# Talking-heads attention and an FFT feed-forward on one core: another order of work where the two stages meet

## The chip, the core and the metric

The kernel runs on one core of a Trainium2 chip. The core has five engines, each with a queue of its own: TensorE (matmuls, PE in the profile, with its weight loads apart as PEld), VectorE (DVE), ScalarE (ACT), GpSimd (POOL) and SyncE (SP), which here only issues transfers. They meet through semaphores. The metric is the device time of one execution in microseconds; of several executions the median counts.

## The reference

All data is float32, except the two feed-forward weights, which come as float64 and are turned into float32 by the kernel itself, bit by bit, on VectorE.

```python
# q, k, v: (8, 12, 448, 64); w_pre, w_post: (12, 12)
scores = scale * q @ k.transpose(0, 1, 3, 2)
scores = einsum('bhij,hg->bgij', scores, w_pre)
attn = softmax(scores)                    # max, exp, sum + 1e-9
attn = einsum('bhij,hg->bgij', attn, w_post)
x = heads_side_by_side(attn @ v)          # (8, 448, 768)

u = x + real(fft(fft(x, axis=1), axis=2))
un = (u - mean(u)) / sqrt(var(u) + 1e-6)  # along the last axis
out = u + relu(un @ w_ch1) @ w_ch2        # w_ch1: (768, 3072), w_ch2: (3072, 768)
```

## The kernel before

**Two stages.** `mix_phase` computes attention and the Fourier part and writes u to memory, into `u_scr` and `u_rev`. `ffn_phase` reads u back in tiles of 512 rows (seven of them, t = 0 to 6), normalises, and does the two products. Both products use a scheme of seven half-size products in place of eight (Strassen's), so each has seven operands per side: ub and w1t for the first, h and w2t for the second, in the order of `ORDER = (0, 4, 5, 1, 6, 2, 3)`. Some operands are sums of others: for ub the four differences in `total`, which come after the others.

**Attention** runs in 192 steps (TOT), 24 to each of the 8 batches. A step computes a pre-mix (L478, tile mx), the row maxima (L485), the exponentials (L492, tile PP), the scaling by the row sums on GpSimd (L502), the post-mix (L512, tile po) and a transpose on VectorE (L523, tile Pv). Which work goes with which step is written out by hand: `ORDERS` gives the order within even and odd steps, and the `AT_...` tables give the step in which each other piece is due. Six steps make a group of 112 rows, four groups a batch. For each group the products with v (L539; 56 matmul instructions for each of three parts, pr = 0, 1, 2) go from PSUM into XT, a tile with a single buffer, through four ScalarE copies a part (the helper's line L330, XT<-ms). In three of the four groups one or two columns of XT have no rows of their own; `done` clears them after the copies of the last part (L561, on GpSimd: 1, 2, 0 and 1 columns for groups 0 to 3). Six TensorE transposes (L572) then turn XT, and two ScalarE copies bring the result into X.

**Folds.** The Fourier part begins with sums and differences of the X of two groups, on GpSimd (L593 to L614): 8 operations for the first pair of groups of a batch and 12 for the second. They go into a list, `folds`, of which each step takes one or two, after its scaling on GpSimd. What is left when the steps are over is taken by `fold_rest`, which `ffn_phase` calls. The products that follow (L637, L653) come later; those of the last batch are dealt out between the products of the first feed-forward tile (`next_part`).

**The seam.** Before the first product (L954), tile t = 0 has to be made ready, for four slices of 128 rows (x = 0 to 3):
- `stats`: means and variances on VectorE (L900, L901);
- `power`: the inverse square roots ("roots"), four small operations on GpSimd (L905 to L908);
- `norm`: un = (u - mean) times root, on ScalarE (L916), two buffers for four slices;
- `turn`: six TensorE transposes a slice (L925) into two PSUM tiles psQ of two buffers, y = 0 and 1, and a ScalarE copy of each (L927) into ub;
- `total`: the four differences of ub on VectorE (L933), and then the stores of all seven ub on SyncE (L937), which later rounds read back;
- the loads of w1t (L881) and w2t (L885) on SyncE, seven of 384 KB each.

**What sets the order.** A planner orders each engine's queue when the program is built, by the place of an instruction in the program and by the time at which its own model takes its inputs to be ready. In a `manual_schedule` region the engines named keep the order in which the program emits their instructions. Where a region's instructions fall among those of another region, though, is left to the planner, and so is the order on engines that a region doesn't name. Attention is one region, for TensorE, VectorE, ScalarE and GpSimd. `stats(0)`, `power(0)` and `fold_rest` are a second, for TensorE, VectorE and GpSimd. Everything behind them is a third, for TensorE and VectorE only: ScalarE's part (un, the copies to ub) and SyncE's transfers are placed by the planner, which may put them between instructions of attention.

Of the kernel before, what the change touches and what calls it, by code (L numbers as in the profile page):

```python
# [16 lines left out]
P = 128  # L17
# [30 lines left out]
TOT = B * GS  # L48
# [5 lines left out]
MG = 4  # L54
# [45 lines left out]
NK = DM // 2 // P  # L100
# [35 lines left out]
def _ap(t: bass.AP, offset: int, dims) -> bass.AP:  # L136
    return bass.AP(tensor=t.tensor, offset=t.offset + offset,
                   ap=[list(d) for d in dims])
# [6 lines left out]
def _row(t: bass.AP) -> int:  # L145
    return t.ap[0][0]
# [144 lines left out]
def mix_phase(ctx, tc, rest, ident, q, k, v, w_pre, w_post, u_scr, u_rev, wts):  # L291
# [6 lines left out]
    nc = tc.nc  # L298
# [28 lines left out]
    pend, folds, later = [], [], []  # L327

    def copy(eng, out, in_):
        (nc.scalar.copy if eng == "a" else nc.vector.tensor_copy)(out=out, in_=in_)  # L330

    def flush():
        while pend:
            pend.pop(0)[1]()
# [7 lines left out]
    def ms_tile():  # L342
        return ms[-1]()
# [115 lines left out]
    def emit_gather(T):  # L459

        Kr = pkr.tile([P, 2, S], F32, name="Kr", tag="Kr")
        Sb = blocks[T // BS]["Sb"]
        row = _row(Sb)
        for z in range(2):
            for x in range(2):
                p0 = MG + 4 * (T % BS) + 2 * z + x
                nc.sync.dma_start(  # L467
                    out=Kr[64 * x:64 * x + KR, z, :],
                    in_=_ap(Sb, p0 * row, [[RS * row, 2 * R], [S, 6], [1, S]]))
        steps[T]["Kr"] = Kr  # L470
# [25 lines left out]
    def emit_scale(T):  # L496
        PP, den = steps[T]["PP"], steps[T]["den"]
        rcp = psm.tile([P, 2], F32, name="rcp", tag="rcp")
        nc.vector.tensor_scalar(rcp[:, :], den[:, :], 1e-9, None, op0=ALU.add)  # L499
        nc.vector.reciprocal(out=rcp[:, :], in_=rcp[:, :])  # L500
        for x in range(2):
            nc.gpsimd.tensor_scalar(PP[:, x, :], PP[:, x, :], rcp[:, x:x + 1], 1.0,  # L502
                                    op0=ALU.mult, op1=ALU.mult)
# [24 lines left out]
    def emit_av(g, pr):  # L528

        st = batches[g["b"]]  # L530
        Pv = g["Pv"]
        rp = _row(Pv)
        nu = GT * 4
        pss = [ms_tile() for _ in range(2)]
        for jb in range(C7):
            for x in range(2):
                for y in range(2):
                    i = 2 * pr + x
                    nc.tensor.matmul(  # L539
                        pss[y][64 * x:64 * x + 64, :nu * R],  # L540
                        st["v", pr][64 * y:64 * y + 64, x, jb * D:(jb + 1) * D],
                        _ap(Pv, 64 * y * rp + 32 * jb + R * i,
                            [[rp, 64], [HS, nu], [1, R]]),
                        start=(jb == 0), stop=(jb == C7 - 1))
        if pr == 0:
            g["XT"] = pxt.tile([P, 6, XW], F32, name="XT", tag="XT")
        XT = g["XT"]
        rx = _row(XT)
        first, sg, none = PLACE[g["gi"]]

        def done(y):
            rs = _row(pss[y])
            for e in range(2):

                o = MG + first + sg * NB * e
                dst = _ap(XT, (3 * y + pr) * XW + o, [[rx, P], [sg * RS, R], [sg, RS]])
                src = _ap(pss[y], 60 * e, [[rs, P], [1, R], [R, RS]])
                copy(ENG["AV"][y], dst, src)
            if y == 1 and pr == 2:
                for o in none:  # L560
                    nc.gpsimd.memset(XT[:, :, MG + o:MG + o + 1], 0.0)  # L561
        return [lambda y=y: done(y) for y in range(2)]

    def emit_x(g):
# [173 lines left out]
    def take(kind, s):  # L738
        large = 0
        while fill[kind] and fill[kind][0][0] <= s:  # L740
            fn = fill[kind].pop(0)[2]
            if kind == "none":
                large += bool(fn())
            elif kind == "full":
                flush()
                pend.extend((1, e, None) for e in fn())
            else:
                room(2)
                evs, n = fn()
                pend.extend((1, e, n) for e in evs)  # L750
        return large

    s = int(min(v_[0][0] for v_ in fill.values()))
    ET = mybir.EngineType
    with tc.manual_schedule(engines={ET.PE, ET.DVE, ET.Activation, ET.Pool}):
        while s <= TOT - GS + AT_X[-1]:
            old = len(later)
            n = take("none", s)
            ahead, now = 0 <= s + LM < TOT, 0 <= s < TOT
            for op in ORDERS[s % 2]:  # L760
                if op == "flush":
                    flush()
                elif op in fill:
                    take(op, s)
                elif op == "conv":
                    if s >= 4:
                        wts.deal(1)
                elif op == "gather":
                    if 0 <= s + LG < TOT:
                        if any(e[2] is not None and e[2] <= (s + LG) // BS for e in pend):  # L770
                            flush()
                        emit_gather(s + LG)
                elif op == "scale":
                    if ahead:
                        emit_scale(s + LM)
                    for _ in range(old):
                        later.pop(0)()
                    for _ in range(min(len(folds), 1 if n and s > 3 else 2)):
                        folds.pop(0)()
                elif op in ("post", "turn"):  # L780
                    if now:
                        (emit_postmix if op == "post" else emit_turn)(s)
                elif ahead:
                    (emit_premix if op == "pre" else emit_max if op[0] == "m"
                     else emit_exp)(s + LM, *map(int, op[3:]))
            s += 1
        flush()
        wts.deal(1000)
# [26 lines left out]
ORDER = (0, 4, 5, 1, 6, 2, 3)  # L815
# [5 lines left out]
def ffn_phase(ctx, tc, rest, ident, u_scr, u_rev, wts, ub_scr, out, fold_rest,  # L821
# [4 lines left out]
    nc = tc.nc  # L826
# [23 lines left out]
    def ps_tile(key):  # L850

        n = taken[key] = taken[key] + 1
        more = len(pps) > 3 and key != "Q" and n % 3 == 0
        return pps[3 if more else "QPR".index(key)].tile(
            [P, 512], F32, name="ps" + key, tag="ps" + key, bufs=1 if more else 2)
# [5 lines left out]
    us, ubs, w1, w2 = {}, {}, {}, {}  # L861
# [21 lines left out]
    def load_w2(c, i):  # L883
        w2[i] = pw2.tile([P, FM, DH], F32, name="w2t", tag="w2t")
        nc.sync.dma_start(out=w2[i][:, :, :], in_=wts.w2[c][i])  # L885
# [5 lines left out]
    UB = {(0, 0): 0, (0, 1): 6, (1, 0): 1, (1, 1): 2}  # L891
# [19 lines left out]
    def norm(t, x):  # L911
        if x == 0:
            for i in (0, 6, 1, 2, 4, 5, 3):
                new_ub(t, i)
        uns[x] = pun.tile([P, DM], F32, name="un", tag="un")
        nc.scalar.activation(uns[x][:, :], us[t][:, x, :], ACTF.Identity,  # L916
                             bias=mvs[t][:, x, 2:3], scale=mvs[t][:, x, 1:2])

    def turn(t, x):
        un = uns.pop(x)  # L920
        for y in range(2):
            ps = ps_tile("Q")
            for c in range(NK):
                cc = NK * y + c
                nc.tensor.transpose(ps[:, c * P:(c + 1) * P],  # L925
                                    un[:, cc * P:(cc + 1) * P], ident[:, :])
            nc.scalar.copy(  # L927
                out=ubs[t, UB[y, x // 2]][:, :, (x % 2) * P:(x % 2 + 1) * P],
                in_=ps[:, :NK * P].rearrange("p (c n) -> p c n", n=P))

    def total(t, n):
        o, a, b = ((4, 6, 0), (5, 2, 4), (6, 2, 6), (3, 1, 5))[n]
# [112 lines left out]
    with tc.manual_schedule(engines={ET.PE, ET.DVE}):  # L1045
        for x in range(NT2):
            norm(0, x)
            turn(0, x)
        for n in range(4):
            total(0, n)  # L1050
        for i in ORDER:
            load_w2(0, i)
        for n in range(NC * NTB):
            c, t = divmod(n, NTB)

            if c + 1 < NC and 0 <= t - (c == 0) < NK + FM:
                wts.add(c + 1, t - (c == 0))
            wts.deal(0)
            if c == 0 and t + 2 < NTB:
                load_u(t + 2)  # L1060
            second(n, first(n))
            wts.deal(1000)
            if n == 0:
                assert not parts
                rest.close()
                pu.append(pool("pu2", side="right"))
                beside.close()
                pps.append(pool("ppy", space=bass.MemoryType.PSUM))
# [61 lines left out]
```

## Time and profile before

The median of three runs is 2419.3 us (2418.86 to 2423.73). The profiled execution:

| | |
|---|---|
| span | 2415.9 us |
| TensorE busy | 2357.9 us (98%) |
| VectorE / ScalarE / GpSimd busy | 1545.1 / 799.1 / 792.6 us |
| attention's last post-mix (L512) begins | 834.1 us |
| the first feed-forward product, L954 | 860.6 us |

The profile's page gives totals over the whole span. The seam is some 25 us of 2416, about 1%, so it doesn't show in the totals. It has to be read from the views that keep the order of time: the timeline of one engine in a window, the chain of waits in that window, and the table of windows, which also gives TensorE's granted clock. In a timeline each row is a start in us, a duration in us, engine, line, operation, tiles written and read, and a count where like instructions follow each other; a bracket gives the time that the engine had stood idle, and what released it.

The group rows for the work that the change touches (time in all, mean in ns, and the idle time before them):

| work | line | engine | count | busy us | mean ns |
|---|---|---|---|---|---|
| clearing of XT | L561 | GpSimd | 32 | 3.2 | 118 |
| folds: pairs | L593 | GpSimd | 64 | 64.4 | 1015 |
| un | L916 | ScalarE | 28 | 28.2 | 1030 |
| transposes of un | L925 | TensorE | 168 | 25.2 | 278 |
| copies to ub | L927 | ScalarE | 56 | 24.8 | 482 |
| totals of ub | L933 | VectorE | 28 | 29.1 | 1043 |

### The profile page before, as it was taken

What the parts mean: (1) busy time and instruction counts of PE and PEld (TensorE: products, weight loads), DVE (VectorE), ACT (ScalarE), POOL (GpSimd) and SP (SyncE); (2) the same over time, 40 slices, a digit from 0 to 9 for tenths busy, and PEclk for the clock granted to TensorE, in tenths of its full rate; (3) what the DMA queues carried; (4) which work ended last, traced back from release to release, by engine and by line L of the source; (5) the groups of instructions that cost most, each with busy time, mean ns of one, the idle gap of its engine ahead of it and who ended that gap; (6) DMA issues with size and microseconds to landing.
All of it is one profiled execution on the core that took longest, in us unless ns stands there. A gap on an engine that the chain in (4) does not pass through costs nothing.

```text
span 2415.9 us, 54667 instructions
## 1 busy us (share of the span) xinstructions
PE 2357.9 (98%) x21680; PEld 1592.4 (66%) x21680; DVE 1545.1 (64%) x3103; ACT 799.1 (33%) x2059; POOL 792.6 (33%) x1293
## 2 busy tenths in 40 slices
PE   6999999999999899999999999999999999999999
PEld 3555555555555477676777777777777777777776
DVE  3878879789897757775667356635664457533333
ACT  4776767676677532321110110110110111111110
POOL 3587877878776531120111011101110011000000
PEclk9999999999999999999999999999999999999999
DMA  6665555656554556336444444534442644353331
GB/s 147 177 177 167 183 170 163 188 164 187 170 175 160 175 194 208 131 139 241 142 137 146 150 146 129 162 124 159 146 153 93 200 133 141 121 170 112 118 118 53
DMA packets 168620, 372.50 MB, mean 154 GB/s; under 512 B 36750, under 2 KB 90022, under 8 KB 168366
## 3 DMA queue, kind: packets, MB, share of 16 engines
q1 hardware_dynamic: 129038, 260.22, 32.5%
q0 software_dynamic: 33760, 107.40, 15.2%
q8 instruction: 173, 2.83, 0.5%
q10 hardware_dynamic: 5568, 1.38, 0.3%
q14 instruction: 81, 0.66, 0.1%
HBM read 211.98 MB, written 74.34 MB: 119 GB/s over the span
## 4 chain that ended last, share of the span: by engine, by line
PE 89%; DMA 4%; DVE 2%; SPq 2%; POOL 2%; ACT 1%; issue 1%; ACTq 0%; DVEq 0%; POOLq 0%
PE psP L954 18%; PE psP L1010 18%; PE psR L954 9%; PE psR L1010 9%; PE mx L478 6%; PE ms L539 5%; PE ms L451 5%; PE po L512 5%; PE psQ L1010 5%; PE psQ L954 5%; DMA Kr<-Sb 3%; PE ms L653 2%; SPq L467 1%; PE ms L426 1%; PE ms L637 1%; PE ms L572 1%
## 5 line engine op out<-in xcount | busy, mean ns | idle before, releaser
L954 PE MATMUL psP<-ub,w1t 128*128 128x256 f32 x2016 | 462.6, 379 | 0.0
L1010 PE MATMUL psP<-w2t,h 128*128 128x384 f32 x1344 | 461.0, 486 | 0.0
L954 PEld LDWEIGHTS psP<-ub,w1t 128*128 128x128 f32 x2016 | 383.1, 190 | 60.4
L213 POOL DMA_DIRECT2D raw<-in_moe_w_ch_dram x120 | 68.9, 574 | 924.8 <-DVE tmp L257 905.8
L1010 PEld LDWEIGHTS psP<-w2t,h 128*128 128x128 f32 x1344 | 254.6, 190 | 165.7
L502 POOL TENSOR_SCALAR PP<-PP,rcp 128x448 f32<-128x448 f32 x384 | 253.9, 670 | 216.9 <-DVE rcp L500 171.4
L492 ACT ACTIVATE PP<-mx,nmx 128x448 f32<-128x448 f32 x384 | 240.3, 631 | 170.9 <-DVE nmx L485 158.5
L485 DVE TENSOR_REDUCE nmx<-mx 128x1 f32<-128x448 f32 x384 | 222.2, 616 | 99.6 <-PE mx L478 98.1
L959 ACT COPY h<-psP 128x512 f32<-128x512 f32 x42 | 24.6, 585 | 764.4 <-PE psP L954 713.1
L1016 DVE TENSOR_TENSOR u<-u,psP 128x384 f32<-128x384 f32 x336 | 183.3, 552 | 141.7 <-PE psP L1010 139.5
L478 PE MATMUL mx<-Kr,kw 60*32 60x448 f32 x3072 | 232.8, 547 | 20.3 <-DMA Kr<-Sb 15.8
L954 PE MATMUL psR<-ub,w1t 128*128 128x256 f32 x1008 | 231.3, 379 | 0.0
L1010 PE MATMUL psR<-w2t,h 128*128 128x384 f32 x672 | 230.5, 486 | 0.0
L965 DVE TENSOR_TENSOR h<-h,psQ 128x512 f32<-128x512 f32 x42 | 28.8, 686 | 298.7 <-PE psQ L954 298.7
L523 DVE STREAM_TRANSPOSE Pv<-po 128x896 f32<-128x896 f32 x192 | 212.3, 1106 | 6.0 <-PE po L512 2.7
L512 PE MATMUL po<-PP,kw 60*32 60x448 f32 x3072 | 211.4, 541 | 4.1 <-DVE rcp L499 2.4
L954 PEld LDWEIGHTS psR<-ub,w1t 128*128 128x128 f32 x1008 | 191.6, 190 | 25.8
L451 PE MATMUL ms<-kT,qT 64*32 64x448 f32 (+1 forms) x3072 | 201.3, 542 | 0.7 <-DVE wrp L366 0.7
L330 ACT COPY Sb<-ms 124x448 f32<-124x448 f32 x384 | 183.6, 541 | 30.9 <-DMA Kr<-Sb 15.0
L539 PEld LDWEIGHTS ms<-Pv,vv 64*64 64x64 f32 x5376 | 144.3, 134 | 69.1 <-issue 35.1
L1010 PEld LDWEIGHTS psR<-w2t,h 128*128 128x128 f32 x672 | 127.3, 190 | 87.3
L539 PE MATMUL ms<-Pv,vv 64*64 64x120 f32 x5376 | 166.8, 270 | 0.0
(92 smaller groups left out, 2819.8 us busy)
## 6 DMA issues: line engine op xcount, KB each, us to landing
ub<-ub SPq DMA_DIRECT2D x294, 384.0 KB
Kr<-Sb SPq DMA_DIRECT2D x768, 105.0 KB
raw<-in_moe_w_ch_dram POOLq DMA_DIRECT2D x72, 256.0 KB, 3.4
raw<-in_moe_w_ch_dram POOLq DMA_DIRECT2D x48, 384.0 KB, 3.7
w<-wst POOLq DMA_DIRECT2D x126, 128.0 KB, 3.1
w<-wst POOLq DMA_DIRECT2D x84, 192.0 KB, 3.3
w1t<-w SPq DMA_DIRECT2D x42, 384.0 KB
w2t<-w SPq DMA_DIRECT2D x42, 384.0 KB
```

The lines of the kernel that those rows point to most:

```text
L330: (nc.scalar.copy if eng == "a" else nc.vector.tensor_copy)(out=out, in_=in_)
L451: nc.tensor.matmul(pss[x][o:o + hi - lo, :S], st["qT", xx][64 * x:64 * x + 64, y, lo:hi], st["kT", xx][64 * x:64 * x + 64, y, :], start=Tr ...
L478: nc.tensor.matmul(mx[x][64 * z + o:64 * z + o + 32, :S], kw1[64 * x:64 * x + KR, o:o + 32], Kr[64 * x:64 * x + KR, z, :], start=True, sto ...
L485: nc.vector.tensor_reduce(nmx[:, :], steps[T]["mx"][x][:, :S], axis=AX.X, op=ALU.max, negate=True)
L492: nc.scalar.activation(steps[T]["PP"][:, x, :], steps[T]["mx"][x][:, :S], ACTF.Exp, bias=steps[T]["nmx", x][:, :], accum_out=steps[T]["den ...
L502: nc.gpsimd.tensor_scalar(PP[:, x, :], PP[:, x, :], rcp[:, x:x + 1], 1.0, op0=ALU.mult, op1=ALU.mult)
L512: nc.tensor.matmul(po[o:o + 32, z, :S], kw2[64 * z:64 * z + KR, y, :], PP[64 * z:64 * z + KR, :, c * HS:(c + 1) * HS], start=True, stop=True)
L523: nc.vector.transpose(g["Pv"][:, T % GT, :].rearrange("p (z s) -> p z s", z=2), steps[T]["po"][:, :, :S])
L539: nc.tensor.matmul(pss[y][64 * x:64 * x + 64, :nu * R], st["v", pr][64 * y:64 * y + 64, x, jb * D:(jb + 1) * D], _ap(Pv, 64 * y * rp + 32 ...
L954: nc.tensor.matmul(p[:, m, :], w1[i][:, kc, m * P:(m + 1) * P], ub[:, kc, :], start=i in OPENS and m == kc == 0, stop=kc == NK - 1, skip_g ...
L1010: nc.tensor.matmul(p, lhs[i][:, kf, x * P:(x + 1) * P], w2[i][:, kf, :], start=i in OPENS and kf == 0, stop=kf == FM - 1, skip_group_check ...
L1016: nc.vector.tensor_tensor(us_, us_, p, op=ALU.add)
```

## The change

It has five parts, all for the seam, except that the first acts throughout attention:
1. The columns of XT without rows are cleared on VectorE instead of GpSimd.
2. In the last three of the 192 steps, and in those after them, no fold is taken from the list. They are left to `fold_rest`, which stands behind the roots on GpSimd; this is to let the roots go first.
3. The first transpose of un is pinned behind everything that the program has emitted for TensorE before it. As the third region keeps TensorE's order, all transposes of un for t = 0, and the products, then come after attention's last instruction on TensorE.
4. For t = 0 the copy of y = 1 goes to VectorE, that of y = 0 stays on ScalarE, so that the two can run side by side.
5. The loads of w2t for the first round are emitted before the totals and their stores.

```diff
             if y == 1 and pr == 2:
                 for o in none:
-                    nc.gpsimd.memset(XT[:, :, MG + o:MG + o + 1], 0.0)
+                    nc.vector.memset(XT[:, :, MG + o:MG + o + 1], 0.0)
...
-                    for _ in range(min(len(folds), 1 if n and s > 3 else 2)):
-                        folds.pop(0)()
+                    if s < TOT - 3:
+                        for _ in range(min(len(folds), 1 if n and s > 3 else 2)):
+                            folds.pop(0)()
...
-                nc.tensor.transpose(ps[:, c * P:(c + 1) * P],
-                                    un[:, cc * P:(cc + 1) * P], ident[:, :])
-            nc.scalar.copy(
-                out=ubs[t, UB[y, x // 2]][:, :, (x % 2) * P:(x % 2 + 1) * P],
-                in_=ps[:, :NK * P].rearrange("p (c n) -> p c n", n=P))
+                tr = nc.tensor.transpose(ps[:, c * P:(c + 1) * P],
+                                         un[:, cc * P:(cc + 1) * P], ident[:, :])
+                if t == x == y == c == 0:
+                    tc.keep_in_program_order(tr)
+            copy = nc.vector.tensor_copy if t == 0 and y else nc.scalar.copy
+            copy(out=ubs[t, UB[y, x // 2]][:, :, (x % 2) * P:(x % 2 + 1) * P],
+                 in_=ps[:, :NK * P].rearrange("p (c n) -> p c n", n=P))
...
             norm(0, x)
             turn(0, x)
+        for i in ORDER:
+            load_w2(0, i)
         for n in range(4):
             total(0, n)
-        for i in ORDER:
-            load_w2(0, i)
```

## The prediction

> **What bounds the kernel now.** I read first the page's chain that ended last, by engine:
>
> ```profile
> PE 89%; DMA 4%; DVE 2%; SPq 2%; POOL 2%; ACT 1%; issue 1%; ACTq 0%; DVEq 0%; POOLq 0%
> ```
>
> TensorE carries 89% of the span, so time is to be had only where TensorE stands still. I then read TensorE's timeline around the seam, where attention ends and the feed-forward part begins:
>
> ```profile
> 836.69 1.56 PE L653 MATMUL ms<-tcs,z 97*113 97x193 f32 x8
> 838.10 0.38 PE L572 MATMUL ms<-ident,XT 128*113 128x128 f32 x2
> 846.40 1.20 PE L572 MATMUL ms<-ident,XT 128*113 128x128 f32 x4 [7.92 <-ACT XT L330]
> 847.53 0.66 PE L539 MATMUL ms<-Pv,vv 64*64 64x120 f32 x2
> 848.12 0.47 PE L925 MATMUL psQ<-ident,un 128*128 128x128 f32 x1
> 848.52 5.73 PE L539 MATMUL ms<-Pv,vv 64*64 64x120 f32 x166
> ...
> 860.60 2.76 PE L954 MATMUL psP<-ub,w1t 128*128 128x256 f32 x12
> ```
>
> Columns are start, duration, engine, line, tiles, count; the bracket is idle time and its releaser. Of group 2's six transposes of XT, two run, and then TensorE stands 7.92 us for a ScalarE copy into XT. ScalarE's and GpSimd's timelines say why that copy was late:
>
> ```profile
> 834.24 0.80 ACT L330 COPY XT<-ms 128x60 f32<-128x60 f32 x4 [4.30 <-PE ms L539]
> 844.07 1.95 ACT L916 ACTIVATE un<-u,mv 128x768 f32<-128x768 f32 x2 [9.04 <-POOL mv L908]
> 845.92 0.78 ACT L330 COPY XT<-ms 128x60 f32<-128x60 f32 x4
> ```
>
> ```profile
> 830.64 1.25 POOL L502 TENSOR_SCALAR PP<-PP,rcp 128x448 f32<-128x448 f32 x2 [3.79 <-DVE rcp L500]
> 832.05 1.04 POOL L676 DMA_INDIRECT v<-X,rows  x1 [0.16 <-issue]
> 833.11 1.97 POOL L593 TENSOR_TENSOR xs<-X 113x384 f32<-113x384 f32 x2
> ...
> 842.03 0.25 POOL L905 TENSOR_SCALAR mv<-mv 128x4 f32<-128x4 f32 x1
> ...
> 843.79 0.24 POOL L908 TENSOR_SCALAR mv<-mv 128x4 f32<-128x4 f32 x1
> ```
>
> Two normalisations (un) stand in ScalarE's queue ahead of the XT copies. They wait for the roots (L905 to L908), and those stand in GpSimd's queue behind eight folds, 833.11 to 841.94. The roots' own input was ready long before:
>
> ```profile
> 834.63 0.21 DVE L901 BATCH_NORM_AGGREGATE mv<-st 128x2 f32<-128x12 f32 x1
> ```
>
> The chain of waits in this window tells another story, which has to be settled:
>
> ```profile
> 838.63 5.61 DMA w1t<-w
> 844.24 0.01 ACTq L916
> ```
>
> It puts the second un down to a weight load that landed at 844.24. But the first un began at 844.07, before that landing and 0.04 after the end of L908 (843.79 + 0.24), and the pair ran in 1.95 us, as two un do at 876.54 also. I take the roots as the wait.
>
> TensorE's clock, by windows (window; length; busy time and count of PE and its weight loads, DVE, ACT, POOL; granted clock; DMA share; GB/s):
>
> ```profile
> 839.00:840.00 1.00, 0.00 (x0) 0.00 (x0) 1.00 (x3) 0.00 (x0) 0.92 (x2) 1.00 0.97 280
> 841.00:842.00 1.00, 0.00 (x0) 0.00 (x0) 0.00 (x0) 0.00 (x0) 0.94 (x3) 0.50 0.96 283
> 850.00:851.00 1.00, 1.00 (x29) 1.00 (x28) 0.00 (x0) 0.00 (x0) 0.00 (x0) 0.56 0.34 123
> 852.00:854.00 2.00, 2.00 (x86) 2.00 (x77) 0.00 (x0) 0.95 (x5) 0.00 (x0) 1.00 0.00 0
> ```
>
> The idle stretch costs twice: until about 851 TensorE then runs at half clock, 29 matmuls per us against 43.
>
> [...] 1.00 at 839, 0.50 from 841, 1.00 from 851, 4.5 us after work resumed. [...] XT copies whose matmuls ended at 836.76 waited until 845.92 behind two un. [...] the four totals (L933) took 6.36 us for 4 beside folds, against a median of 0.95 each.
>
> **The change part by part.**
>
> *Folds held back (s < TOT - 3).* The eight folds of steps 189 to 192 go to fold_rest, which stands behind power(0) on GpSimd. The roots then start when the last statistics are done, 834.84, with GpSimd free since 833.09, and take what they took, 842.03 to 844.03 = 2.0: done at 836.9. The two un run 836.95 to 838.9. If ScalarE keeps the order un, un, XT, the copies start at 838.85, and the transposes follow 0.48 behind (846.40 - 845.92): 839.3. TensorE's idle stretch, from 838.48, falls from 7.92 to 0.85: **-7.1**. If the planner now puts the copies first, they run at 836.8 and the gap is gone: -7.9. I take -7.1. The folds then run 836.9 to 845.7 (8.8 us); the next ones need group 3's X, not due before about 845.5. They cost nothing: GpSimd was idle from 844.03 to 847.66 and again to 854.62.
>
> *Clock.* A gap of 0.85 doesn't halve the clock if a stretch from 838.48 to between 840 and 841 was needed for it. The four transposes take 4 x 0.14 (six in 0.82 at 823.50) instead of 1.20: **-0.6**. The 168 attention matmuls take between 168 / 43 = 3.9 and their present 6.65 (847.60 to 854.25, with the inserted transpose). I take 4.2: **-2.4**.
>
> *The pin on the first transpose.* It keeps L925 behind all attention work. The single L925 at 848.12 (about 0.4 inside the 6.65, counted above) moves behind. Queued behind the pin is the whole turn(0, x) chain, and L954 behind that. Between L925 and L572 nothing overlaps any more: up to **+0.6**.
>
> *Copies shared with VectorE.* Before, ScalarE has after 854.31 four XT copies (0.8), two X copies (1.05), eight ub copies (8 x 0.48, overlapping to about 3.5) and two un (1.95), and is busy nearly without gap until 861.28; L954 starts 6.35 after the matmuls' end at 854.25. Four ub copies leave for VectorE, idle 20.69 us there. Nearest row: its PSUM copy of 128x384 to kT, 0.543. What stays on ScalarE is about 5.6, but un 2 and 3 still need the transposes of un 0 and 1, and the last transposes need un 3: placed one after another, L954 starts 5.7 to 6.4 after the end, without the pin's cost double. Taken with the pin: **-0.2** (range -1 to +1).
>
> *w2 loads ahead of the totals' stores.* In the SyncE queue a ub store sits from 841.75 to 857.23 waiting for ScalarE, and six of seven w2t loads come at 867.73 and later. They now go earlier. Their readers (L1010) start at 883.72 without a wait: 0. They can't delay L954 unless they take bandwidth from w1t; those loads, issued 837.27 to 841.70, keep the DMA busy until about 847.5, and L954 is due at about 850.
>
> *Clearing on VectorE.* 32 memsets leave GpSimd (0.118 each). GpSimd's memset held TensorE once for long:
>
> ```profile
> 460.56 0.91 PE L572 MATMUL ms<-ident,XT 128*113 128x128 f32 x6 [2.92 <-POOL XT L561]
> ```
>
> GpSimd was late there with other work too (the scale behind it ended at 461.71, and the post-mix that needs it began at 462.57), so of 2.9 I count 1. VectorE gains 32 x 0.112 (its memset of kw) = 3.6 us of work, bounds 0 and 3.6 on the path; with 2% of the chain on VectorE I count 0.5. Sum **-0.5**.
>
> Sum: -7.1 - 0.6 - 2.4 - 0.2 - 0.5 = -10.8; from 2419.3: **2408.5**. Everything behind L954 moves as a block, since TensorE is full from there on.
>
> **Rivals.**
> 1. *The un go further ahead.* With earlier roots the planner may put both un before the XT copies of 834.24 as well. Then these run at 838.9, the L653 block (which needs their buffer) at 839.4 to 840.9, transposes to 841.7; TensorE has idled from 836.76, the clock drops, the 168 take 6.1: 847.8, and L954 follows 6.35 later at 854.2 instead of 860.6: **2412.9**. For it: un already overtook one set of copies. Against: even then the order is bounded by the last statistics.
> 2. *The wait is not the roots but w1t*, as the chain has it, or the early w2 loads delay w1t. Then un or L954 wait till where they are now, and only about 1 us is won: **2418**. Against: the first un's start, above.
> 3. *VectorE stalls in attention.* If each clearing has to wait for the four XT copies (0.80) before it, and VectorE's queue (max, transpose, reciprocals) stands behind it: 24 places x 0.8 = 19.2, less the seam's 10.3: **2428**, slower. For it: at 80.86 the memset began 0.08 after the last copy. Against: VectorE itself waited for TensorE until 80.86 there, so such a wait would mostly lie in idle time.
>
> **Chances.** The forecast 0.62; rival 1 0.18; rival 2 0.08; rival 3 0.07; still better (no gap, ScalarE's relief in full, the whole 2.9: about 2404.5) 0.05. Faster by over 0.2% (under 2414.5): 0.62 + 0.18 + 0.05 = 0.85; within 0.2%: 0.08; slower: 0.07. The range takes in rival 1 with its spread and the better case, and leaves out the other two: 2404.5 to 2414.5.
>
> **What would show it.** Right: L905 at about 835, before the folds; TensorE's gap at 838.5 under 1.5 us; clock 1.00 throughout 838 to 852; no L925 among L539; w2t issued before 857; L954 first at about 850. Wrong: un still started by a DMA near 844; clock at 0.50 in spite of a short gap; VectorE waiting for XT copies in attention, so that L954 is late although the gap is gone.

## The result and the profile after

The changed kernel takes 2405.83 us (median of 4 runs, 2401.92 to 2409.85) against 2419.08 (4 runs, 2415.22 to 2423.73): ratio 0.9945, 95% interval 0.992 to 0.9969. A second comparison of the same two kernels, on another occasion, gave 2410.36 (6 runs) against 2419.83 (51 runs): ratio 0.9961, interval 0.9947 to 0.9976, or 9.4 us with 5.8 to 12.8. The kernel is faster, by somewhere near 10 us; the 13.3 us between the first two medians have a wide interval of their own (7.5 to 19.4).

In the code after the change the lines move a little: the transposes of un are L927 (L925 before), un is L918, the copies to ub L934, the statistics L902 and L903, the roots L907 to L910, the first product L960 (L954 before). In the kernels further below that change ScalarE's order they move again: there the transposes of XT are L574 (L572 before).

First TensorE's timeline of the changed kernel at the seam (start, duration, engine, line, tiles, count; in brackets idle time and releaser):

```profile
836.30 1.57 PE L653 MATMUL ms<-tcs,z 97*113 97x193 f32 x8
837.70 0.38 PE L572 MATMUL ms<-ident,XT 128*113 128x128 f32 x2
840.08 1.10 PE L572 MATMUL ms<-ident,XT 128*113 128x128 f32 x4 [1.99 <-ACT XT L330]
841.10 5.83 PE L539 MATMUL ms<-Pv,vv 64*64 64x120 f32 x168
...
848.06 0.82 PE L927 MATMUL psQ<-ident,un 128*128 128x128 f32 x6
...
852.50 2.76 PE L960 MATMUL psP<-ub,w1t 128*128 128x256 f32 x12
```

The wait of 7.92 us is down to 1.99, the attention products run as one block (5.83 us; before, with a transpose of un among them, 6.72), and the first feed-forward product starts at 852.50 instead of 860.60. GpSimd's timeline shows why: the roots now follow the last scaling and the store, ahead of the folds.

```profile
831.80 1.26 POOL L502 TENSOR_SCALAR PP<-PP,rcp 128x448 f32<-128x448 f32 x2 [3.78 <-DVE rcp L500]
833.21 1.04 POOL L676 DMA_INDIRECT v<-X,rows  x1 [0.15 <-issue]
835.69 0.25 POOL L907 TENSOR_SCALAR mv<-mv 128x4 f32<-128x4 f32 x1 [1.44 <-DVE mv L903]
...
837.46 0.25 POOL L910 TENSOR_SCALAR mv<-mv 128x4 f32<-128x4 f32 x1
837.68 1.95 POOL L593 TENSOR_TENSOR xs<-X 113x384 f32<-113x384 f32 x2
```

ScalarE's order is what it was, two un and then the copies into XT; both are just earlier:

```profile
834.67 0.81 ACT L330 COPY XT<-ms 128x60 f32<-128x60 f32 x4 [3.57 <-PE po L512]
837.74 1.95 ACT L918 ACTIVATE un<-u,mv 128x768 f32<-128x768 f32 x2 [2.26 <-POOL mv L910]
839.60 0.78 ACT L330 COPY XT<-ms 128x60 f32<-128x60 f32 x4
```

The table of windows (granted clock is the third number from the end) shows that the clock fell even so:

```profile
839.00:840.00 1.00, 0.00 (x0) 0.00 (x0) 0.85 (x2) 0.97 (x4) 0.92 (x2) 1.00 1.02 353
841.00:842.00 1.00, 1.00 (x21) 0.90 (x24) 0.06 (x1) 0.53 (x2) 1.00 (x3) 0.50 0.94 292
844.00:846.00 2.00, 2.00 (x84) 2.00 (x80) 0.00 (x0) 1.22 (x7) 1.84 (x4) 1.00 1.05 409
```

**A measure for the seam.** From the first feed-forward product to the end, all 14 profiles of this study take 1555.3 to 1556.4 us; so what follows the seam only moves. What comes before it scatters: GpSimd's last scaling (L502) begins anywhere from 822.7 to 840.4 us. So I measure from the start of that scaling, which lies ahead of the statistics, the last post-mix and everything that the change touches at the seam, to the start of the first product. Before: 860.60 - 830.64 = 29.96 us. After: 852.50 - 831.80 = 20.70. The difference is 9.26 us, and agrees with the whole time of the larger comparison (9.4). It also shows a flaw in starting from the end of group 2's products, as the first expectations below do. In the profile of before, TensorE lost 1.15 us in the second-last block of products, ahead of that point, and this was mostly hidden in the wait that followed (timeline of TensorE, first before, then after):

```profile
831.33 2.85 PE L539 MATMUL ms<-Pv,vv 64*64 64x120 f32 x56
```

```profile
832.05 1.70 PE L539 MATMUL ms<-Pv,vv 64*64 64x120 f32 x56
```

The reason is the clock: TensorE had stood still for 2.36 us just before, and the granted clock was 0.50 from 830.39 to 833.81. In the profile after, a stop of 2.44 us at the same place was followed by no drop. What decides between the two the profiles don't show.

M is read from one profile of each kernel. The two profiles of the changed kernel agree to 0.11 us, and the kernel that only clears on VectorE, with the seam of before, has 30.24 against 29.96. The intervals of the whole times are 5 to 12 us wide, so they can't confirm differences in M of one or two us among the variants of the changed kernel.

### The profile page after: what moved, and what is told of

Its sections match the earlier page's. It is cut to its first block, busy times and chain, and to the rows that moved or that the text cites. A ratio compares the mean times of both kernels' runs of the same rounds, so it can differ in the third digit from the quotient of the medians.

```text
span 2408.1 us, 54666 instructions
## 1 busy us (share of the span) xinstructions
PE 2358.0 (98%) x21680; PEld 1590.1 (66%) x21680; DVE 1540.5 (64%) x3139; ACT 799.6 (33%) x2055; POOL 791.5 (33%) x1261
## 4 chain that ended last, share of the span: by engine, by line
PE 89%; DMA 4%; DVE 2%; SPq 2%; ACT 1%; POOL 1%; issue 1%; ACTq 0%; DVEq 0%; POOLq 0%
PE psP L960 18%; PE psP L1016 18%; PE psR L960 9%; PE psR L1016 9%; PE mx L478 6%; PE ms L539 5%; PE ms L451 5%; PE po L512 5%; PE psQ L1016 5%; PE psQ L960 5%; DMA Kr<-Sb 3%; PE ms L653 2%; SPq L467 1%; PE ms L426 1%; PE ms L637 1%; PE ms L572 1%
## 5 line engine op out<-in xcount | busy, mean ns | idle before, releaser
L960 PE MATMUL psP<-ub,w1t 128*128 128x256 f32 x2016 | 462.5, 379 | 0.0
L960 PEld LDWEIGHTS psP<-ub,w1t 128*128 128x128 f32 x2016 | 382.8, 190 | 60.7
L502 POOL TENSOR_SCALAR PP<-PP,rcp 128x448 f32<-128x448 f32 x384 | 254.0, 671 | 219.4 <-DVE rcp L500 173.2
L960 PE MATMUL psR<-ub,w1t 128*128 128x256 f32 x1008 | 231.3, 379 | 0.0
L960 PEld LDWEIGHTS psR<-ub,w1t 128*128 128x128 f32 x1008 | 191.4, 190 | 25.9
```

The lines of the kernel that those rows point to most:

```text
L960: nc.tensor.matmul(p[:, m, :], w1[i][:, kc, m * P:(m + 1) * P], ub[:, kc, :], start=i in OPENS and m == kc == 0, stop=kc == NK - 1, skip_g ...
```

## The experiments

Comparisons are always with the kernel before, in the same rounds. "Seam" in the text on record of the first eight means the interval that ends at the same first product but starts at group 2's last product; what I report is the measure just defined, called M.

**The changed kernel again** (no edit).

> The changed kernel once more, on the chip and in the rounds of the next three. Measure of the seam: from the end of the last attention product of group 2 (L539) to the first feed-forward product; before 836.76 to 860.60 = 23.84 us, after 836.36 to 852.50 = 16.14. Theory (the fold order moves the roots ahead, nearly all of the gain is in the seam): seam 16.1 again, whole time 7 to 9 us under the kernel before. Rival (clearing on VectorE wins as much again in attention, as the medians, 13.3 apart, would allow): whole time 12 us or more under it, with the last attention product of group 2 ending 4 us earlier than before.

Ratio 0.9961 (0.9947 to 0.9976), M = 20.81. The theory's 7 to 9 us is at the low side of 9.4, the rival's 12 is only just inside the interval, and the 9.26 of M needs no gain in attention. The second profile brings something new. The clock stayed at 1.00 this time, with a gap of 2.10 us, and the products took 4.94 us instead of 5.83. Yet M is no shorter, since TensorE then stood still in front of the very last transpose of XT (timeline of TensorE, this run):

```profile
842.29 4.94 PE L539 MATMUL ms<-Pv,vv 64*64 64x120 f32 x168
...
849.55 0.27 PE L572 MATMUL ms<-ident,XT 128*113 128x128 f32 x1 [1.18 <-ACT X L330]
```

The ScalarE copy that the bracket names had ended at 848.67, and the weight load of this transpose had run at 848.14, so, as far as the profile shows, the instruction was waiting for neither. More on this hole below.

**Only the folds held back.**

```diff
-                    for _ in range(min(len(folds), 1 if n and s > 3 else 2)):
-                        folds.pop(0)()
+                    if s < TOT - 3:
+                        for _ in range(min(len(folds), 1 if n and s > 3 else 2)):
+                            folds.pop(0)()
```

> The kernel before with one part of the change: no fold taken from the list from step 189 on. Theory: the roots start about 0.1 us after the last statistics, un about 2 us later, TensorE's gap falls from 7.9 to about 2, seam 16 to 17.5 us, whole time 6 to 8 us under before. Rival (un waits for the first w1t load, as the chain of waits had it): un still starts near 844 and the seam stays at 23.8, whole time within 1 us of before. Rival (the gain needs the pin and the shared copies): seam 20 or more.

Ratio 0.9977 (0.9966 to 0.9989), or 5.6 us (2.7 to 8.2); M = 22.68, 7.28 less than before. The roots start 0.09 us after the last statistics, un at 838.20, and TensorE's gap is 2.11. So this one part carries most of the gain, and the roots, not w1t, are what un waited for. What is missing to 20.70 shows itself in part. The clearing of XT on GpSimd now stands behind all eight folds, and TensorE waits for it (a row of GpSimd's timeline and one of TensorE's):

```profile
846.92 0.12 POOL L561 MEMSET XT<- 128x6 f32 x1
```

```profile
847.09 0.47 PE L572 MATMUL ms<-ident,XT 128*113 128x128 f32 x2 [0.68 <-POOL XT L561]
```

**Only the clearing on VectorE.**

```diff
-                    nc.gpsimd.memset(XT[:, :, MG + o:MG + o + 1], 0.0)
+                    nc.vector.memset(XT[:, :, MG + o:MG + o + 1], 0.0)
```

> The kernel before with one part of the change: the columns of XT cleared on VectorE. Theory: the seam stays at 23.8, and attention gains 0.5 to 1 us at most: whole time 0 to 2 us under before. Rival (the clearing wins in attention): 4 to 6 us under. Rival (VectorE stalls for the XT copies): 2 us or more over.

Ratio 0.9996 (0.9984 to 1.0007), from 3.9 us faster to 1.7 slower; M = 30.24. By itself it does nothing that can be measured. Beside held-back folds it takes away the wait of 0.68 us just shown.

**The changed kernel with the folds back in the last steps.**

```diff
-                    if s < TOT - 3:
-                        for _ in range(min(len(folds), 1 if n and s > 3 else 2)):
-                            folds.pop(0)()
+                    for _ in range(min(len(folds), 1 if n and s > 3 else 2)):
+                        folds.pop(0)()
```

> The changed kernel with the folds taken in the last steps as before; pin, shared copies, early w2 loads and clearing stay. Theory: roots behind the folds again at about 842, TensorE's gap 7.5 to 8 us, seam 22.5 to 23.8, whole time 0 to 2 us under before. Rival (the other parts carry a good share): seam 20 or less, 4 us or more under before.

M = 29.38: the pin, the shared copies, the early loads and the clearing give 0.6 us as long as the roots stand behind the folds. TensorE's row has the old wait:

```profile
853.15 1.20 PE L572 MATMUL ms<-ident,XT 128*113 128x128 f32 x4 [9.51 <-ACT XT L330]
```

The whole time says 0.9982 (0.9971 to 0.9994), or 1.5 to 7.0 us faster, more than M accounts for. Whether the remainder is attention with the clearing on VectorE or only attention's scatter stays open.

**The changed kernel without the pin.**

```diff
-                if t == x == y == c == 0:
+                if False:
                     tc.keep_in_program_order(tr)
```

> The changed kernel without the pin on the first transpose of un; TensorE's order at the seam is then the one of before, one L925-type transpose among the attention products and eight among the transposes of XT. Theory (the pin matters little on its own): tail from the last attention product to the first feed-forward product 5.5 to 7 us (with the pin 5.57 and 6.84 in two profiles), seam 16 to 18, time within 2 us of the changed kernel. Rival (without the pin the mixed order costs, as in the folds-only kernel, whose tail was 8.40): tail 8 us or more.

Ratio 0.9945 (0.9925 to 0.9965); M = 21.61, 0.9 over the changed kernel, with one transpose of un among the products again. Of the 0.9 us, 0.6 comes from ahead of the pinned work: here the statistics themselves ended 0.6 us later after the scaling (4.42 against 3.80), in a profile in which the clock was at half from 829.32 to 832.73. That leaves 0.3 us or so for the pin. In this profile there was also a hole of 1.41 us, so even that isn't shown, and the whole time can't tell.

**The changed kernel with late w2t loads.**

```diff
-        for i in ORDER:
-            load_w2(0, i)
         for n in range(4):
             total(0, n)
+        for i in ORDER:
+            load_w2(0, i)
```

> The changed kernel with the w2t loads behind the totals and their stores again. Theory A (the early loads do nothing for the seam): seam 16.1 to 16.3 as with them, time the same. Theory B (they fill the DMA engines at the seam, [...]): DMA share at the first 5 us after the attention products low, no such hole, tail 5.6, time up to 1 us under the changed kernel. Rival (they were needed): the second products wait for w2t, the stretch behind the first product longer than 1555.6 us.

Ratio 0.9951 (0.9935 to 0.9967); M = 20.90, 0.2 from the changed kernel. Nothing waits for w2t: behind the first product 1555.4 us as ever. There was no hole in this profile, but the products took 6.43 us against 4.94 in the one with the hole of 1.18, so it doesn't decide for theory B.

**The changed kernel with un 0 and 1 behind the XT copies** (ScalarE order only).

```diff
+                last = copy(ENG["AV"][y], dst, src)
+                if g is groups[-2] and pr == 2 and y == e == 1:
+                    MARK.append(last)
...
+        if t == 0 and x < 2:
+            tc.add_manual_dep(un.ins, MARK[-1].ins.name, NoSync ...)
```

> The changed kernel with one edit more: the first two un are ordered behind the last copy into XT of group 2 on ScalarE (order only, no wait). Theory (the gap of 2.0 us left in the changed kernel is ScalarE standing in front of the XT copies for the roots, and it is what still halves the clock): TensorE's gap 0.3 us or less, clock 1.00 throughout, the 168 attention products in 3.9 to 4.4 us, seam 12 to 13, time 2.5 to 4 us under the changed kernel. Rival (un is then late itself, and the tail grows by what the gap shrinks): seam 15 or more. Rival (the clock drops anyway): seam 13.5 to 14.5.

The gap in front of the transposes is gone, as expected. But M = 20.66: nothing is won. TensorE's timeline says where it went:

```profile
835.83 0.42 PE L539 MATMUL ms<-Pv,vv 64*64 64x120 f32 x2
837.51 4.64 PE L539 MATMUL ms<-Pv,vv 64*64 64x120 f32 x166 [1.27 <-ACT X L330]
...
844.63 0.27 PE L574 MATMUL ms<-ident,XT 128*113 128x128 f32 x1 [1.34 <-issue]
```

The two un now stand in front of the two X copies, whose PSUM tile the second product needs: a wait of 1.27 us in place of the old one. And the hole is back, 1.34 us, this time with no releaser at all; it ended at 844.63, and the clock was at half from 844.98 to 848.39. Ratio 0.995 (0.9935 to 0.9964). Counted as in the expectation the seam is 16.13, as the first rival had it (15 or more), but only part of the way it named: the tail from the last attention product did grow, from 5.57 to 7.73, of which the hole is 1.34. Neither the theory nor a rival named the wait for X or the hole.

**The same with four buffers for un in the first tile.**

```diff
-    pun = pool("pun", 2)
+    pun = pool("pun", 1)
...
-        uns[x] = pun.tile([P, DM], F32, name="un", tag="un")
+        uns[x] = pun.tile([P, DM], F32, name="un", tag=f"un{x if t == 0 else x % 2}")
```

> As the kernel before it in this list, and with four buffers for un of the first tile, so that all four un can run before the transposes of the first. Theory (the tail of 5.6 us is ScalarE's un 2 and un 3 between its copies): tail 4.0 to 4.6 us, seam 11 to 12, time 3.5 to 5 us under the changed kernel. Rival (the tail is set by the transposes, the copies and the two psQ tiles): tail 5.2 or more, time as the kernel before it in this list.

Ratio 0.995 (0.9931 to 0.9968), but M = 22.67, worse by 2. Only un 0 and 1 have an order imposed. With buffers of their own, two un (2 and 3, by that order) went ahead of the XT copies, and the other two behind them and ahead of the X copies. So the gap of 2.01 us was back, a wait of 0.78 for the X copies came on top, and the clock was at half for 6.83 us. The question about the tail is answered all the same. All four un had run before the last attention products, the clock was full again and there was no hole, and still the tail is 5.43 us against 5.57, as the rival had it (5.2 or more). From the last transpose of XT to the first product it is 4.15 us against 4.28 in the changed kernel. So un 2 and un 3 between the copies do not set the tail.

**The changed kernel with all copies to ub on ScalarE.**

```diff
-            copy = nc.vector.tensor_copy if t == 0 and y else nc.scalar.copy
+            copy = nc.scalar.copy
```

> The changed kernel with all eight copies to ub on ScalarE again. Measure from here on: from the start of GpSimd's last scaling (L502) to the first feed-forward product; 29.96 us before, 20.70 and 20.81 for the changed kernel in two profiles. Theory (VectorE's four copies relieve ScalarE, which sets the tail): tail from the last attention product to the first feed-forward product 6.3 to 7 us against 5.57, measure 21.4 to 22.2. Rival (un 2 and un 3, not the copies, set the tail): tail 5.4 to 5.8, measure as in the changed kernel.

Ratio 0.9964 (0.9948 to 0.998); M = 21.76, 1.0 over the changed kernel, as expected. From the last transpose of XT to the first product it takes 5.09 us against 4.28, at full clock in both: VectorE's copies are worth 0.8.

**ScalarE's order written out, w2t late.** Un 0 and 1 behind both X copies of group 2, un 2 and 3 behind the XT copies of parts 1 and 2 of group 3, four buffers.

```diff
+                if g is groups[-1] and pr and y == e == 1:
+                    MARK[pr + 1] = last
...
+                if g is groups[-2] and u == 1:
+                    MARK[0] = MARK[1] = last
...
+        if t == 0 and x in MARK:
+            tc.add_manual_dep(un.ins, MARK[x].ins.name, NoSync ...)
```

The lines for four buffers and for the late w2t loads are as in the edits above.

> The changed kernel with ScalarE's order at the seam written out: un 0 and 1 behind both X copies of group 2, un 2 behind the XT copies of group 3's part 1, un 3 behind those of part 2, four buffers for un in the first tile; and the w2t loads late as in the kernel before. Theory (the gap, the clock and the tail are all ScalarE's order): no gap above 0.5 us before the attention products, clock 1.00, products in about 5 us, tail 4 to 4.6, measure 16 to 16.8, time 4 us under the changed kernel. Rival ([...]): a hole of about 1.3 us marked as issue right behind the products, measure 17.3 to 18. Rival (w1t lands too late for so early a start): the first products wait for w1t, measure 18 or more.

M = 18.28, the shortest of all, 2.4 us under the changed kernel. The ratio to before, 0.994 (0.9923 to 0.9957), is the lowest of the study, but not apart from the changed kernel's (0.9945 and 0.9961): the whole time doesn't show that this order is faster. Group 2's transposes and the products follow each other without a gap, at full clock, and then the hole comes, here 0.79 us:

```profile
841.56 0.82 PE L574 MATMUL ms<-ident,XT 128*113 128x128 f32 x6
842.31 4.96 PE L539 MATMUL ms<-Pv,vv 64*64 64x120 f32 x168
847.21 0.47 PE L574 MATMUL ms<-ident,XT 128*113 128x128 f32 x2
848.15 0.58 PE L574 MATMUL ms<-ident,XT 128*113 128x128 f32 x3 [0.47 <-ACT XT L330]
849.52 0.27 PE L574 MATMUL ms<-ident,XT 128*113 128x128 f32 x1 [0.79 <-ACT un L925]
```

The 0.47 in front of it is my own order: un 2 (846.73 to 847.76) stood before the last XT copies. So the theory's 16 is missed by the hole, by this, and by a stretch of transposes no shorter than before.

**The same with early w2t loads.**

```diff
-        for n in range(4):
-            total(0, n)
         for i in ORDER:
             load_w2(0, i)
+        for n in range(4):
+            total(0, n)
```

> As the kernel before it in this list, but with the w2t loads early. Theory [...] (the hole of 0.8 us in the folds-only kernel with late w2t loads, and of 1.2 to 1.4 us in three kernels with early ones[...]): hole 0.5 us longer than with late loads. Rival (the hole has nothing to do with the loads): the same hole in both.

Ratio 0.9947 (0.9928 to 0.9965); M = 20.37; a hole of 1.33 us. Of the 2.1 us to the kernel with late loads, 0.5 is the hole. The rest was lost ahead of group 3: the end of group 2's products lies 6.12 us after the scaling here and 4.56 there. Here the clock was at half from 837.04 to 840.45, after a stop of 2.05 us; there it was full. With no wait left to hide it, such a drop goes straight into M: in this profile little more than 0.3 us is left of the gain over the changed kernel.

**The same with two buffers.** Only un 0 is ordered behind the X copies; un 1 follows it by itself.

```diff
-    pun = pool("pun", 1)
+    pun = pool("pun", 2)
...
-        uns[x] = pun.tile([P, DM], F32, name="un",
-                          tag=f"un{x if t == 0 else x % 2}")
+        uns[x] = pun.tile([P, DM], F32, name="un", tag="un")
...
-        if t == 0 and x in MARK:
+        if t == 0 and x == 0:
```

> As the kernel before it in this list (early w2t loads), but with two buffers for un, so that un 2 and un 3 must wait for the transposes of un 0 and un 1. Theory (buffers set the tail): tail 5.5 to 6 us without a hole, about 1.2 us more than with four. Rival (the two psQ tiles and their copies set it): tails alike.

Ratio 0.9957 (0.9942 to 0.9973); M = 19.45; hole 1.36 us. From the last transpose of XT to the first product it is 5.09 us, against 4.15 with four buffers, but the clock was at half here from 855.58 to 858.99, so this pair can't tell buffers from clock. At full clock two buffers give 4.28 (the changed kernel) and four give 4.15 (the kernel above with four buffers, in which only un 0 and 1 are ordered). The theory asked for about 1.2 us between them, so the buffers are not what sets this stretch.

**The hole.** It stands, in seven profiles, right behind the 168 attention products: 0.79 us in the two with late w2t loads (folds only; order written out), and 1.18, 1.33, 1.34, 1.36 and 1.41 in the five with early ones. It is there whenever the products took under 5.3 us (in one case apart from a wait of 1.27), and in none of the seven profiles in which they took 5.8 or more. In the profile after, where they took 5.83 and the clock was at half from 840.22 to 843.63, TensorE came by that place with no stop longer than 0.17 us. In the two profiles of the changed kernel and the one of its form with late w2t loads M was 20.70, 20.81 and 20.90, although the products took 5.83, 4.94 and 6.43 us: faster products gained nothing there.

What holds TensorE in the hole is not shown. In the kernel with un behind the XT copies it stands as "issue" (1.34 us), in the second profile of the changed kernel under a copy that had ended 0.88 us before. Why it is shorter in the two kernels with late loads is open as well: the DMA engines were about as busy around it there (shares of 0.95 and 0.99 over 2 us) as in the other five (1.00 to 1.03).

## Why the prediction was right, and where it was not

The forecast was 2408.5 us, 10.8 less than before. The runs give 13.3 and 9.4 less, the seam 9.26; some 4 us of the 13.3 lie outside the seam (see the clearing, below). By its steps, with the seam cut where the prediction cut it:

- **Folds and roots: right.** The roots began 0.09 us after the last statistics and took 2.0; un followed at once, in the old order. Counted from the scaling, group 2's transposes resumed at 840.08 - 831.80 = 8.28, against 846.40 - 830.64 = 15.76 before: 7.48 won, 7.1 forecast. From the last statistics to the transposes it took 4.48 us (forecast 839.3 - 834.84 = 4.46); the other 0.4 came from upstream, where the statistics ended 3.80 us after the scaling instead of 4.20. Folds alone gave 7.28 of M, and without them the rest gave 0.6. The gap was nevertheless 1.99, not 0.85: the copies came no later than forecast, but TensorE came earlier, group 2's products ending 4.57 after the scaling instead of 6.12, as the clock had not dropped ahead of them. A gap was the wrong thing to forecast: its end was set by ScalarE, its start by something else.
- **Clock and products: half right, the term mis-sized.** The forecast was 0.6 + 2.4 = 3.0. From the resumed transposes to the end of the products it took 7.85 us before and 6.85 after: 1.0. Two things failed. The clock dropped right behind a stop of 1.99 us, from 840.22 to 843.63, and the products took 5.83 (forecast 4.2). That a gap well under that of before leaves the clock alone was the author's estimate: in the profile of before the clock had fallen at 840.63, only 2.15 us after TensorE stopped, and how short a stop is short enough no trace showed. And where the clock did stay full, in the second profile of the changed kernel, this stretch took 5.59, 2.3 less than before, but the hole of 1.18 followed and M was no shorter. The forecast couldn't see the hole: the trace that it was read from has none, with the clock at half up to 850.87 and the products in 6.72 us.
- **Pin, shared copies, tail: right within its range.** Forecast -0.2 with -1 to +1. From the end of the products to the first feed-forward product 6.35 before, 5.57 after: -0.78. VectorE's copies have a part in it: without them the end of this stretch, from the last transpose of XT, takes 5.09 instead of 4.28. A copy took 0.56 us (forecast 0.543).
- **w2t loads: nothing for the time, as forecast.** They were issued at 841.67 to 848.83 and nobody waited. M changes by 0.2. In the written-out order the hole was 1.33 us with early loads and 0.79 with late ones, one profile each.
- **Clearing: its size not settled, its place missed.** Forecast -0.5 in attention; -1.0 measured with -3.9 to +1.7. The VectorE memset takes 0.063 us, not 0.112. What is seen of it is at the seam, 0.68 us beside held-back folds, which the forecast did not count. A gain in attention as well is not ruled out: of twelve comparisons with this clearing eleven gained more in the whole time than in M, by 2.6 us in the mean of all twelve, while the folds alone gained 1.7 less. But they share their runs of the kernel before in part, and each M is one profile, so this is not shown.
- **The rivals.** Un did not go further ahead. W1t was not the wait: it was the chain's attribution alone, since with only the folds held back un began at 838.20, as soon as its roots were done. In the profile after, the chain puts the second un down to a load of u, again a transfer among its semaphores. VectorE does wait for the XT copies before a clearing, but only as the waits of the clearing-only kernel show (us in total, times, longest):

```profile
DVE XT L561 <- ACT XT L330: 1.8, 3, 0.9
```

That is 1.8 us in three of the places, where rival 3 put 0.8 on each of 24. Before all other clearings but one, which waited 7.5 us for a transpose of XT at the seam, VectorE did not stand idle.

The three stretches follow each other, so they are bound to add up: -7.48 - 1.00 - 0.78 = -9.26. The one term of the sum that was far off is that of clock and products, by 2.0 us. That the total still came close is in part luck: the first and the third stretch won 1.0 us more than forecast.

## What to carry to other kernels

Where two stages meet, look in each queue for work that is not due yet and stands in front of work that the bounding engine waits for: here eight folds on one engine held up the roots, the roots held up un on the next, and un held up four short copies that TensorE needed. Forecast the time at which the bounding engine can resume, counted from a common event upstream, rather than the length of its gap. And taking one wait away shows the next: closing the gap entirely gave nothing. With un's place among all of ScalarE's copies written out, M fell by 2.4, 0.3 and 1.3 us in three kernels, one profile each, instead of the four expected, and the whole times don't show it. A difference of one or two us between two profiles can be no more than a drop of the clock that comes in the one and stays away in the other (2.85 against 1.70 us for the same 56 products, above).

## What the runs showed of the hardware that was not expected

The clock can drop after a short stop, and one kernel can show it in one profile and not in the next. In the changed kernel, right behind a stop of 1.99 us at the transposes of XT, the granted clock was 0.50 from 840.22 to 843.63; in its second profile, with a stop of 2.10 us at the same place, it was 1.00 in every window from 829 to 846. In the kernel of before it was 0.50 from 830.39 to 833.81, right behind a stop of 2.36 us, and from 840.63, within the stop of 7.92, to 850.87. In the profile after, a stop of 2.44 us ahead of the second-last block of products was followed by no drop. With four buffers for un the stop was 2.01 us and the clock at half for 6.83; with only the folds held back it was 2.11, and the 166 products behind it took 4.63 us, against 5.73 in the profile of before. With un behind the XT copies the clock fell at 844.98, 0.35 us after a hole of 1.34 us had ended. So the length of the stop alone doesn't tell the profiles with a drop from those without one. What does is not shown.

TensorE stood still for 0.79 to 1.41 us close behind the 168 products in the seven profiles in which these took under 5.3 us, and in none of the seven in which they took 5.8 or more. The view of waits doesn't name the cause; it shows as "issue" (1.34 us with un behind the XT copies), or under a releaser that had finished before (a copy that ended at 848.67, for a transpose that began at 849.55, in the second profile of the changed kernel).
